# A third of each chunk's output products issued ahead, ten drains of TensorE removed, and a new order of all steps, in a delta-rule attention with a multiplicative feed-forward block

## The chip, the cores and the metric

The kernel runs on one core of a Trainium2 chip. The metric is the device time of one execution in microseconds (us). The kernel before took 578.32 us as the median of three runs (575.9 to 579.85). A profile shows one execution; times inside it are counted from its first instruction.

The engines are named as in the profile: PE is TensorE's matmul, PEld its load of weights (the stationary operand), DVE is VectorE, ACT is ScalarE, POOL is GpSimd, SP is SyncE, which here issues nearly all DMA transfers. A "q" behind an engine is its sequencer.

## The reference

Two blocks follow each other. The first is a delta-rule recurrence over 768 tokens for 4 batches of 8 heads with 48 features each; the second takes its output as 3072 tokens of 384 features.

```python
k_n = k / (np.linalg.norm(k, axis=-1, keepdims=True) + 1e-06)
for t in range(S):                       # S = 768
    kt, vt, bt = (k_n[:, :, t], v[:, :, t], beta[:, :, t, None])
    y[:, :, t] = np.einsum('bhd,bhde->bhe', q[:, :, t], state)
    v_old = np.einsum('bhde,bhd->bhe', state, kt)
    state = state + bt[:, :, :, None] * np.einsum('bhd,bhe->bhde', kt, vt - v_old)
x = y.transpose(0, 2, 1, 3).reshape(B * S, H * D)      # 3072 x 384
a = x @ w1                               # 384 x 1024
b = x @ w2                               # 384 x 1024
out = ((a * b) @ w3) @ w_out             # 1024 x 1024, 1024 x 384
```

q, k, v and beta come as 32-bit floats, the four weights as 64-bit floats, which the kernel turns into 32-bit floats on the chip.

## The kernel before

**Chunks.** The 768 tokens are 12 chunks of 64. Within a chunk the recurrence is written with matrices: scores between keys, the inverse of a triangular matrix made of them, and products with a state of 48 x 48 per batch and head that is handed from chunk to chunk. Two chunks make a pair u = 0 to 5 of 512 tokens for the feed-forward block.

**Steps.** Every piece of work is a Python generator that issues some instructions and then yields. A name in the string `ORDER` runs the generator of that name to its next yield, so `ORDER` is the program's order, written out by hand as some 1380 names. A name called past the generator's last yield does nothing. At the end `in_text_order` (L184) ties the instructions of each engine to that order, so each engine works through its own instructions strictly in the sequence of the text; between engines only semaphores hold, where data or a buffer demand it. The steps that matter here, with m a chunk and u a pair:

- `P0` to `P35` (`piece`, L758): load a piece of a 64-bit weight into one of five `raw` buffers (SP), convert it with two ScalarE operations, one VectorE and one GpSimd operation. P0-P7 are w_out, P8-P23 w3, P24-P35 w1 and w2. `t` transposes a piece of w3, `f` (`fold`, L833) multiplies w3 with w_out in two halves.
- `k`, `q`, `v`, `p`: loads of a chunk. `K`, `Q` and `d`: keys and queries transposed to features by tokens. `g`, `N`: norms of the keys.
- `s` (L426; `first_scores` for the first two chunks): for each half of a chunk's batches one group of products (L436, L442) and two VectorE evictions, U (L448) and PT (L459). `u` writes U to memory.
- `V` (`inverse`, L482): the inverse of two chunks together, 31 steps of two VectorE operations each (L502, L507), between a load `Ub<-Ud` and a store `Vd<-Vb`. For the first two pairs it works in a PSUM pair.
- `e` (`corner`, L538): loads the inverse's blocks (TT and T22), transposes one (L543) and completes the off-diagonal block with two groups of products (L560), each evicted by two ScalarE operations (L576, L587).
- `c` (`chain`, L605): three groups of products (L613): keys with the state, evicted as R (L647); R with the inverse, evicted as X (L658); X with the keys, evicted as the new state S (L679). R, X and S are one VectorE operation each.
- `y` (`outputs`, L685): the chunk's outputs, 64 matmuls in one step, of which 32 take X and PT ("of the tokens") and 32 take the state before the chunk and the queries, 16 for each of two halves z. A matmul of 32-bit floats is two instructions, so the profile shows 64 and 2 x 32. All 64 accumulate into one pair of banks. ScalarE then copies the pair into xT (L736), and six transfers move a part of xT between partitions (L747).
- `b`, `a` (`ab`, L850) and, for the last pair, `a50` to `a53` (`features`, L978): products with w1 and w2 (L857, L997), evicted by ScalarE and by a multiplication on VectorE (L869, L873).
- `S`, `o`, `x` (L916, L1066, L1114): sums of slabs on GpSimd (L930), seven groups of 16 products with the folded weights (L1089), and the results' additions and stores (L1118). Seven products take the place of eight, with sums beside them.

**PSUM.** There are eight banks. Four single banks turn under the tag "f" (`bank`, L172), two pairs under the tag "w" (`two_banks`, L169). `in_turn` (L141) gives the next index of the tag, and passes over an index that is in the set `held`; whoever gets a buffer waits until its last reader is done. Scores, corner, chain and outputs take their banks from "w"; weights, transposes, features and `o` take theirs from "f". The kernel before puts an index into `held` only in `inverse` for the first two pairs.

**The drain.** In `outputs` the products are in two lists: the first holds the state's products of half 0 and all products of the tokens, the second the state's products of half 1. Between the two lists TensorE drains:

```python
for mode, todo in enumerate(modes):
    if mode:
        drain = pe.drain().ins
    for h, z, r, lhs, rhs in todo:
        i = pe.matmul(region(h, z, r), lhsT=lhs, rhs=rhs, ...)
        issued[mode].append(i.ins)
        n += 1
for i in issued[0]:
    in_order(i, drain)
for i in issued[1]:
    in_order(drain, i)
```

Of the kernel before, what the change touches and what calls it, by code (L numbers as in the profile page):

```python
# [44 lines left out]
P14 V0 V0 V0 f0 P15 P15 P19 t11 f2 V0 P14 P14 V0 V0 V0 f1 f5 P23 P23 t6 V0 P15 P15 P23 t11 f5 f5 P23
t15 t15 h0 t7 f7 f7 t7 t6 f3 f3 V0 q2 P17 V0 V0 V0 V0 V0 V0 V0 V0 V0 P17 V0 k2 V0 V0 P16 P17 P28 P17
t9 P16 P24 v1 P16 P16 V0 V0 V0 V0 P28 P20 P28 P28 V0 g1 f3 t9 t8 k3 e0 f7 N0 N0 K2 h0 t8 f4 K2 P20
P20 e0 P20 t12 e0 K2 K2 t12 K2 Q2 n1 e0 e0 n0 n0 e0 P26 g1 f4 Q2 c0 Q2 Q2 f4 g1 g1 f6 Q2 n1 c0 c0
P24 P21 P24 P24 P21 P21 P21 c0 P26 P26 P26 g1 y0 y0 e1 e1 t13 K3 e1 t13 f6 K3 K3 K3 g1 e1 e1 f6 P29
g1 P25 g1 g1 P25 g1 K3 P25 y0 c1 c1 P25 b3 e1 c1 P27 b1 c1 y1 b3 P27 P27 b1 s2 P32 P32 b2 y1 b2 N1  # L50
s2 N1 N1 q3 Q3 P32 P27 P29 P29 s2 s2 Q3 Q3 P29 b4 P31 s2 s2 Q3 Q3 s3 s3 s3 s3 b4 y1 a01 P31 s3 u2
P32 V1 b6 s3 b0 a07 b0 P31 c1 a01 a04 b6 b7 a04 a07 c1 u3 V1 V1 V1 V1 V1 a05 a05 b5 b5 b7 a00 a06
a03 a02 c2 P30 a00 V1 V1 V1 V1 V1 V1 P30 P30 P30 P31 b3 V1 a06 a03 b1 a01 k4 P33 a02 V1 b0 V1 V1 P33
V1 V1 P33 P33 P34 V1 V1 b3 a00 V1 V1 V1 a01 b1 P34 b0 V1 a03 P34 P34 P35 P35 P35 P35 a04 b2 T V1 T
a00 V1 V1 V1 a03 V1 V1 V1 a06 T V1 k5 V1 V1 V1 V1 b5 V1 p4 a04 v2 n2 n2 b2 b4 b7 a06 b6 b5 a02 d4 b6
b4 p4 b7 a07 T a02 o0 a07 V1 e2 e2 e2 c2 e2 a05 e2 e2 c2 g2 g2 g2 g2 g2 g2 g2 e3 e3 e3 v3 e3 S0 g2
g2 a05 o0 x0 o0 d4 d4 d4 c2 y2 v4 x0 x0 S0 y2 g2 c2 S0 N2 p5 N2 k6 S0 o0 c2 n3 e3 e3 n3 c3 c3 N2 S0
S0 S0 S0 o0 S0 S0 S0 S0 S0 S0 S0 x0 c3 o0 c3 y3 s4 S0 x0 x0 o0 s4 y3 s4 s4 p5 x0 d5 d5 d5 d5 s5 s4
y3 u4 s4 s5 x0 s5 s5 s5 u5 a10 x0 V2 x0 x0 s5 a10 a12 a12 a12 a17 a17 a16 a12 a16 V2 V2 n4 V2 V2 V2
# [5 lines left out]
N3 x1 v8 x1 S1 o1 V3 x1 k9 V3 V3 V3 V3 V3 V3 x1 a27 a27 a22 a22 x1 a25 a25 V3 a23 V3 V3 a23 k8 p8 p8
V3 V3 V3 V3 V3 V3 V3 V3 a26 a26 a26 V3 V3 V3 a22 a26 a20 a20 a20 V3 V3 V3 V3 V3 V3 V3 V3 a21 a21 a22
d8 V3 g4 g4 g4 g4 g4 g4 g4 V3 a20 a27 a21 a21 a27 a24 a23 a24 c6 e6 e6 e6 g4 g4 g4 a25 d8 p9 e6 e6
e6 a24 c6 d8 d8 s8 a23 o2 v7 n7 N4 n8 n8 a25 N4 s8 c6 y6 s8 a24 o2 S2 c6 S2 y6 e7 e7 e7 x2 o2 e7 c6
e7 e7 x2 c7 S2 S2 o2 s8 p9 n7 c7 c7 S2 S2 S2 S2 o2 S2 x2 s8 s8 c7 d9 d9 S2 S2 y7 y7 u8 S2 S2 d9 S2
S2 d9 x2 o2 N4 s9 S2 x2 x2 s9 s9 s9 o2 s9 V4 s9 k11 c7 c7 y7 a32 a32 u9 x2 c8 x2 c8 V4 x2 a36 x2 a34  # L70
a34 a36 v10 a33 p10 a31 V4 a31 V4 V4 x2 V4 a33 a37 V4 V4 a30 v9 p10 V4 a37 a30 V4 V4 V4 V4 V4 V4 n9
n9 V4 V4 V4 V4 V4 V4 V4 V4 V4 V4 V4 V4 V4 V4 V4 a35 a35 a33 a33 V4 a35 a32 a30 V4 V4 V4 e8 d10 k10
e9 a32 a34 a30 a35 a36 e8 a31 e8 V5 a37 e8 e8 d10 p11 e8 d10 d10 p11 a34 S3 a36 g5 a31 S3 S3 o3 c8
e9 e9 g5 g5 x3 a37 o3 c8 c8 g5 c8 S3 e9 e9 o3 e9 c9 S3 g5 g5 g5 S3 g5 g5 S3 c9 S3 c9 S3 x3 o3 S3 S3
S3 g5 N5 S3 c9 y8 x3 S3 o3 d11 d11 y9 S3 d11 x3 o3 y8 d11 s11 S3 y9 y9 n10 n10 x3 x3 x3 x3 W x3 s11
s11 s11 s11 u11 s11 o3 x3 x3 s10 s10 s10 s10 s10 u10 s10 N5 N5 a47 a47 a47 a43 V5 a43 a42 a47 a40
a46 a45 V5 V5 V5 V5 V5 V5 V5 a42 V5 V5 V5 V5 V5 V5 V5 V5 V5 V5 V5 V5 V5 V5 a46 V5 V5 V5 a41 V5 V5
a40 a41 V5 V5 a44 a44 a44 V5 V5 a45 a40 V5 V5 a45 a44 e10 e11 a40 a46 c9 c9 a41 a43 c10 a45 e10 e10
a42 W W W W W a43 W W c10 v11 n11 n11 a41 e10 e10 a46 e10 S4 a42 o4 x4 e11 e11 o4 S4 S4 S4 S4 S4 S4
# [1197 lines left out]
```

## Time and profile before

| | |
|---|---|
| median of three runs | 578.32 us (575.9 to 579.85) |
| the profiled execution's own time | 578.96 us |
| its span, first to last instruction | 577.2 us |
| mean granted clock of TensorE | 0.979 |
| PE busy | 539.0 us, 8588 matmuls |
| PEld busy | 393.7 us |
| DVE busy | 340.6 us, 795 instructions |
| ACT busy | 144.8 us, 289 instructions |
| POOL busy | 171.6 us, 217 instructions |
| memory traffic | 43.09 MB read, 11.01 MB written, 94 GB/s over the span |

A line of the timeline or of a group names the line of the kernel, the engine, the operation, then the tile written and the tiles read, the shapes and the count. In a group's line there follow the busy time in all, the mean of one instruction in ns, and the idle time of the engine ahead of these instructions with what ended it. A matmul's end is modelled: matmuls overlap, so the time from one start to the next says how fast they issue. A wait is put down to the operation that ended it last.

### The profile page before, as it was taken

The page shows a single profiled execution, that of the slowest core. Times are in us where ns is not written, and L with a number is a line of the kernel's source. Part 1 is how long each engine was busy: PE and PEld are TensorE (multiplying, and loading weights), DVE is VectorE, ACT ScalarE, POOL GpSimd, SP SyncE. Part 2 cuts the span into 40 slices and gives each one's busy share as a digit, 9 for nine tenths or more (in the row PEclk, how much of TensorE's full clock was granted, in tenths as well). Part 3 has the DMA queues.
Part 4 walks back from the last instruction along what each step waited for, and adds up shares of the span by engine and source line. Part 5 has one row for each costly group of instructions (what it writes and reads, how often), then busy time and mean ns, then how long its engine had stood idle before and what let it go on. Part 6 is the DMA issues. An engine that isn't in the chain of part 4 may idle for free.

```text
span 577.2 us, 19704 instructions
## 1 busy us (share of the span) xinstructions
PE 539.0 (93%) x8588; PEld 393.7 (68%) x8588; DVE 340.6 (59%) x795; ACT 144.8 (25%) x289; POOL 171.6 (30%) x217
## 2 busy tenths in 40 slices
PE   4868998899899999998999999999999999989997
PEld 4734666787689744598744699444886446978897
DVE  6628824649774659865696616795455793123552
ACT  1766466534021011030111130110310102112210
POOL 7544253212838010431211090011840004810000
PEclk9579999999999999998999999999999999999999
DMA  9789964659564481534562534735504105010001
GB/s 183 231 268 257 202 158 117 147 125 172 101 111 79 74 158 32 102 49 74 134 102 65 76 53 76 151 43 110 75 13 91 37 36 85 17 50 8 0 1 55
DMA packets 202806, 56.57 MB, mean 98 GB/s; under 512 B 189952, under 2 KB 196096, under 8 KB 202720
## 3 DMA queue, kind: packets, MB, share of 16 engines
q1 hardware_dynamic: 200608, 54.92, 46.1%
q8 instruction: 67, 1.10, 0.8%
q10 hardware_dynamic: 2112, 0.39, 0.4%
q14 instruction: 19, 0.16, 0.1%
HBM read 43.09 MB, written 11.01 MB: 94 GB/s over the span
## 4 chain that ended last, share of the span: by engine, by line
PE 67%; DVE 13%; DMA 9%; SPq 5%; issue 3%; ACT 2%; POOL 1%; ACTq 0%; DVEq 0%; POOLq 0%
PE ps_f L857 26%; PE ps_f L1089 19%; DVE tb L502 5%; PE ps_w L613 5%; PE ps_f L997 4%; PE ps_w L718 4%; DMA raw<-in_moe_w_dram 3%; DVE ps_w L507 3%; PE ps_w L997 2%; PE ps_w L560 2%; DVE Vb L507 2%; PE ps_w L436 1%; PE ps_w L442 1%; SPq L762 1%; PE ps_f L366 1%
## 5 line engine op out<-in xcount | busy, mean ns | idle before, releaser
L857 PE MATMUL ps_f<-xT,w2s 128*128 128x512 f32 (+1 forms) x288 | 107.8, 525 | 4.0 <-DVE ab L873 2.6
L857 PE MATMUL ps_f<-xT,w1s 128*128 128x512 f32 (+1 forms) x288 | 107.3, 525 | 1.1 <-POOL w1s L777 0.6
L857 PEld LDWEIGHTS ps_f<-xT,w2s 128*128 128x128 f32 x288 | 53.7, 190 | 51.2 <-issue 42.8
L857 PEld LDWEIGHTS ps_f<-xT,w1s 128*128 128x128 f32 x288 | 53.7, 190 | 48.1 <-issue 43.2
L930 POOL TENSOR_TENSOR ab<-ab 128x256 f32<-128x256 f32 x80 | 55.5, 727 | 39.0 <-DVE ab L873 36.8
L1089 PE MATMUL ps_f<-w,ab 128*128 128x192 f32 x320 | 57.1, 332 | 1.6 <-DVE osb L1118 1.3
L869 ACT COPY ab<-ps_f 128x512 f32<-128x512 f32 (+1 forms) x48 | 23.8, 515 | 131.2 <-PE ps_f L857 121.4
L1089 PEld LDWEIGHTS ps_f<-w,ab 128*128 128x128 f32 x320 | 51.6, 190 | 2.8 <-issue 1.9
L836 PE MATMUL ps_f<-wo,w3T 128*128 128x384 f32 x128 | 46.0, 514 | 4.5 <-ACT w3T L830 3.6
L502 DVE TENSOR_TENSOR tb<-Vb,Ub 128x31 f32<-128x31 f32 (+15 forms) x124 | 43.4, 350 | 9.1 <-DMA Ub<-Ud 5.1
L507 DVE TENSOR_TENSOR Vb<-Vb,tb 128x31 f32<-128x31 f32 (+15 forms) x124 | 43.5, 351 | 4.3
L599 POOL TENSOR_TENSOR vtok<-vtok,n 128x384 f32<-128x384 f32 x24 | 19.6, 836 | 80.9 <-DMA vtok<-in_v_dram 78.0
L1089 PE MATMUL ps_f<-room,ab 128*128 128x192 f32 x240 | 43.0, 332 | 0.0
L873 DVE TENSOR_TENSOR ab<-ab,ps_f 128x512 f32<-128x512 f32 (+1 forms) x48 | 27.0, 589 | 21.5 <-PE ps_f L857 21.5
L836 PEld LDWEIGHTS ps_f<-wo,w3T 128*128 128x128 f32 x128 | 24.8, 200 | 21.2 <-issue 5.6
L1089 PEld LDWEIGHTS ps_f<-room,ab 128*128 128x128 f32 x240 | 38.6, 190 | 0.9
L298 POOL TENSOR_TENSOR sq<-ktok 128x384 f32<-128x384 f32 x24 | 19.7, 837 | 58.0 <-DMA out_dram<-osb 20.0
L576 ACT COPY T<-ps_w 32x512 f32<-32x512 f32 x24 | 13.8, 575 | 78.0 <-PE ps_w L560 55.3
L736 ACT COPY xT<-ps_w 112x256 f32<-112x256 f32 x48 | 14.3, 382 | 68.1 <-PE ps_w L718 68.1
L777 POOL TENSOR_TENSOR w<-w,raw 128x512 uint32<-128x512 uint32 x16 | 20.7, 1303 | 29.4 <-DVE w L775 17.6
L502 DVE TENSOR_TENSOR tb<-ps_w,Ub 128x31 f32<-128x31 f32 (+15 forms) x62 | 21.1, 340 | 4.3 <-ACT ps_w L496 2.7
L442 PE MATMUL ps_w<-KQ 48*64 48x64 f32 x640 | 23.5, 228 | 0.1
(148 smaller groups left out, 782.2 us busy)
## 6 DMA issues: line engine op xcount, KB each, us to landing
raw<-in_moe_w_dram SPq DMA_DIRECT2D x16, 512.0 KB, 6.5
vtok<-in_v_dram SPq DMA_DIRECT2D x24, 192.0 KB, 4.1
raw<-in_moe_w_dram SPq DMA_DIRECT2D x24, 192.0 KB, 3.9
out_dram<-osb SPq DMA_DIRECT2D x46, 96.0 KB, 2.5
ktok<-in_k_dram SPq DMA_DIRECT2D x44, 96.0 KB, 3.4
Ud<-U SPq DMA_DIRECT2D x48, 64.0 KB, 2.1
raw<-in_moe_w_out_dram SPq DMA_DIRECT2D x8, 384.0 KB, 5.6
Ub<-Ud SPq DMA_DIRECT2D x6, 512.0 KB, 4.1
```

The costliest lines, as they stand in the source:

```text
L442: pe.matmul(ps[half(z ^ j), 1, n + C * j : n + C * j + C], lhsT=x[:, 0, :], rhs=x[:, j, :], start=True, stop=True,)
L502: dve.tensor_tensor(out=tv, in0=V[:, 0 : s + 1, s : s + 1].to_broadcast([P, s + 1, n]), in1=U[:, s, s + 1 : BS].unsqueeze(1).to_broadcast( ...
L507: dve.tensor_tensor(out=o, in0=o, in1=tv, op=ALU.subtract)
L613: pe.matmul(out(ps, r, h, z), lhsT=lhs(r, h, z), rhs=rhs(r, h, z), start=True, stop=True,)
L718: i = pe.matmul(region(h, z, r), lhsT=lhs, rhs=rhs, start=part[n] not in part[:n], stop=part[n] not in part[n + 1 :],)
L836: pe.matmul(ps[:, 0:DM], lhsT=w3Ts[jc, kc // 4][:, kc % 4 * P : kc % 4 * P + P], rhs=wo(kc), start=(kc == 0), stop=(kc == KF - 1),)
L857: pe.matmul(ps[:].rearrange("p b c t -> p b (c t)"), lhsT=w[:, m, js], rhs=x[:, m, :, c0:c1].rearrange("p b c t -> p b (c t)"), start=(m = ...
L869: act.copy(out=t, in_=ps)
L873: dve.tensor_tensor(out=t, in0=t, in1=ps, op=ALU.mult)
L930: (dve if u == last else pool).tensor_tensor(out=o_, in0=x_, in1=y_, op=op)
L997: pe.matmul(ps[:, j, :], lhsT=w[j], rhs=x, start=first and j == 0, stop=j == 1, skip_group_check=not first,)
L1089: pe.matmul(ps[b][:, b, :], lhsT=ab_of(u, HF * f + i, t0), rhs=ws_[w][:, i], start=first and i == 0 and (b == 0 or n == "F"), stop=i == HF ...
```

## The change

`outputs` is written anew. For chunks 2 to 11 (`ahead`) it has one step more. The first step takes a pair of banks, puts it into `held` and issues the state's products of half 1. The second step issues all products of the tokens and then the state's products of half 0 into the same pair, with no drain. The third is the copies to xT, after which `held` is emptied. Chunk 1 does both groups in one step, with a drain in between; chunk 0 has no state and no drain. The products and their number are the same.

`ORDER` is replaced as a whole: the same steps with the ten new ones, 1389 names instead of 1379, differently mixed. Some places of it are shown below in both versions.

```diff
-V0 beta beta beta k0 g0 g0 g0 K0 K0 k1 K1 g0 g0 K0 K0 K1 K0 s0 g0 g0 g0 g0 K1 K1 K1 q0 Q0 Q0 Q0 g0
-N0 Q0 P8 P8 P8 q1 s0 s0 Q1 P8 s1 P12 P12 P12 Q1 Q1 Q1 Q1 h1 P12 P13 P13 Q0 t0 t4 P13 P13 t5 P10 P10
-P9 P9 P18 P18 P11 u0 P11 t0 t4 s1 s1 P0 P0 P10 P10 P9 P9 P18 P18 h0 t1 t2 t10 P11 t5 P11 t3 P0 P0 P2
+V0 beta beta P8 k0 P8 q0 k1 beta g0 K0 K0 g0 P11 P8 P18 P11 g0 K1 g0 g0 g0 g0 g0 K0 P12 g0 P18 q1
+P12 P11 g0 K1 Q0 K1 Q0 P2 P18 P2 P8 N0 P0 Q0 s0 P2 P0 s1 Q1 t0 P11 t3 P18 s0 P9 P2 P12 s0 P9 P10
+P0 P12 t0 Q1 P9 P10 P3 P1 s1 P10 P3 s1 h0 P0 t4 P3 P13 u1 Q1 t10 P9 P13 P1 t4 P7 P10 P13 h0 t3 P3
...
-N3 S1 c4 o1 S1 e5 S1 c4 y4 S1 S1 N3 S1 c4 p7 S1 d7 x1 p7 o1 y4 e5 e5 c4 d7 d7 d7 s7 s7 s7 s7 s7 s7
-c5 c5 c5 c5 s6 s6 s6 s6 s6 o1 u7 s6 y5 y5 v6 n6 n6 c5 x1 x1 o1 u6 c5 c6 V3 S1 V3 x1 y5 S1 x1 V3 S1
+S1 x1 e5 g3 c4 y4 S1 S1 p7 d6 e5 g3 c4 g3 c4 o1 N3 S1 Q3 S1 p7 S1 v6 y4 o1 d7 N3 y4 S1 n6 x1 S1 V3
+c4 e5 d7 x1 d7 c4 d7 e5 S1 o1 s7 s7 S1 S1 s7 s7 c5 s7 s7 c5 y5 c5 c5 s6 s6 S1 s6 s6 s6 o1 y5 N3 S1
...
-c10 S4 S4 S4 S4 S4 e11 e11 o4 x4 x4 e11 S4 c10 c10 S4 S4 S4 o4 y10 c10 c11 c11 y10 o4 x4 c11 c11 y11
-o4 x4 x4 o4 y11 y11 a50 X5 X5 x4 x4 X5 x4 x4 a51 a52 x4 a50 a50 a50 a50 a50 a50 a50 a50 a50 X5 a50
+e10 c10 x3 e10 a42 S4 e10 c10 S4 o4 W S4 e10 W S4 S4 x4 e11 W e11 e10 y10 e11 S4 o4 S4 S4 e11 c10
+c10 o4 e11 n11 e11 y10 S4 x4 o4 c10 y10 c10 c11 y11 o4 c11 x4 S4 c11 c11 S4 y11 S4 x4 S4 o4 y11 x4
...
     def outputs(c):
-        PT, St, X, KQ = PTs[c], Ss.get(c), Xs[c], KQs[c]
+        St, KQ = Ss.get(c), KQs[c]
         py = two_banks()
+
+        ahead = c > 1
+        if ahead:
+            held.add(("w", turns["w"]))
...
+        if c == 0:
+            accumulate(of_tokens(), True, True)
+        else:
+            issued = accumulate(of_state(1), True, False)
+            if ahead:
+                yield
+            else:
                 drain = pe.drain().ins
-            for h, z, r, lhs, rhs in todo:
...
-        for i in issued[0]:
-            in_order(i, drain)
-        for i in issued[1]:
-            in_order(drain, i)
+                for i in issued:
+                    in_order(i, drain)
+            issued = accumulate([*of_tokens(), *of_state(0)], False, True)
+            if not ahead:
+                for i in issued:
+                    in_order(drain, i)
         yield
...
+        if ahead:
+            held.clear()
         yield
```

`of_state(z)` and `of_tokens()` list the products as before, and `accumulate(todo, first, last_)` issues a list and marks the first and last product of each part of the banks as start and stop only where the list is the first or the last of the chunk.

More of the change, by code (lines that the diff above doesn't have):

```diff
@@ L45 @@
[L45 to L59, printed above, removed]
@@ L65 @@
[L65 to L79, printed above, removed]
```

94 lines of the change are left out of this document (64 added, 30 removed).

## The prediction

> **What bounds the kernel now.** I read the page first: span and busy shares.
>
> ```profile
> span 577.2 us, 19704 instructions
> ...
> PE 539.0 (93%) x8588; PEld 393.7 (68%) x8588; DVE 340.6 (59%) x795; ACT 144.8 (25%) x289; POOL 171.6 (30%) x217
> ```
>
> TensorE is idle for 577.2 - 539.0 = 38.2 us. Second, the busy time by stage (length of the stretch, then busy TensorE) says where.
>
> ```profile
> 101.30:150.00 48.70, 44.54 (x727) 36.56 (x724) 33.98 (x91) 19.14 (x42) 14.15 (x13) 1.00 0.74 147
> 150.00:571.00 421.00, 411.63 (x6421) 297.85 (x6421) 246.65 (x557) 69.18 (x142) 107.95 (x145) 1.00 0.36 67
> ```
>
> It idles 4.2 us from 101.3 to 150 and 9.4 us from there to 571. The other 24.6 us lie in the front, where the weights arrive, and in the last stores. Third, whom TensorE waited for (us in total, times, longest):
>
> ```profile
> PE ps_f L857 <- DVE ab L873: 2.6, 2, 1.3
> PE ps_f L857 <- POOL w2s L777: 1.4, 2, 0.9
> PE ps_w L613 <- DVE R L647: 1.4, 1, 1.4
> PE ps_f L1089 <- DVE osb L1118: 1.3, 1, 1.3
> PE ps_w L613 <- issue: 1.0, 1, 1.0
> PE ps_w L613 <- ACT TT L587: 1.0, 2, 0.7
> PE ps_w L718 <- DVE X L658: 0.7, 1, 0.7
> PE ps_w L436 <- DVE PT L459: 0.4, 1, 0.4
> PE ps_w L436 <- ACT TT L587: 0.3, 1, 0.3
> ```
>
> Behind the front the kernel is TensorE's own work with a dozen short waits. Six rows (L613, L718, L436) are small products of the recurrence that wait for their data or for the eviction of a "w" pair of banks: 1.4 + 1.0 + 1.0 + 0.7 + 0.4 + 0.3 = 4.8 us. A new order can win no more here than the waits hold, but it can add waits.
>
> **The change, part by part: the drains.** One chunk's output products on TensorE (start, duration), and the group row with the 216 ns of one product:
>
> ```profile
> 349.82 0.66 PE L718 MATMUL ps_w<-KQ,S 48*48 48x64 f32 x32
> 350.31 1.08 PE L718 MATMUL ps_w<-PT,X 64*48 64x64 f32 x64
> 351.50 0.66 PE L718 MATMUL ps_w<-KQ,S 48*48 48x64 f32 x32
> 352.10 2.87 PE L1089 MATMUL ps_f<-room,ab 128*128 128x192 f32 x16
> ```
> ```profile
> L718 PE MATMUL ps_w<-PT,X 64*48 64x64 f32 x768 | 13.3, 216 | 0.9 <-DVE X L658 0.7 <-issue 0.2
> ```
>
> The first 32 take 350.31 - 349.82 = 0.49 us of issue. The last of the 64 starts at 350.31 + 1.08 - 0.22 = 351.17, so a product could follow at 351.19; it comes at 351.50: a drain costs 0.31 us, and ten go, -3.1. The last 32 take 0.60 before a large product, 0.11 more than the first 32. The third that goes ahead is now a group of its own and may pay that 0.11 as well, 0 to +1.1 for ten; I take the middle, since such groups stand before small and before large products. Together **-2.6** (bounds -3.1 and -2.0). [...]
>
> **The hold.** With a third ahead, a pair of banks is held from y's first step to its copies. There are two pairs: meanwhile every product of chain, corner and scores takes the other, each behind the eviction of the one before. Nothing overtakes a waiting product: all of TensorE's queue stands behind it. Rows give the price of such a hand-over:
>
> ```profile
> 505.52 1.15 PE L613 MATMUL ps_w<-R,TT 64*64 64x48 f32 x64
> ...
> 506.49 0.63 PE L718 MATMUL ps_w<-KQ,S 48*48 48x64 f32 x32
> 506.81 0.96 DVE L658 TENSOR_TENSOR X<-ps_w,wt 128x768 f32<-128x768 f32 x1 [0.55 <-PE ps_w L613]
> 507.82 1.10 PE L718 MATMUL ps_w<-PT,X 64*48 64x64 f32 x59 [0.70 <-DVE X L658]
> ```
>
> L613 has issued by 506.49 and TensorE has X at 507.82: **1.33 us** for one VectorE operation of the chain (R, X or S), less what TensorE has in between (here 32 products, 0.49).
>
> ```profile
> 260.58 0.30 PE L436 MATMUL ps_w<-KQ 48*64 48x128 f32 x1
> ...
> 260.83 1.18 ACT L587 ACTIVATE TT<-ps_w 32x512 f32<-32x512 f32 x2 [3.09 <-PE ps_w L560]
> ...
> 261.81 0.69 DVE L448 TENSOR_TENSOR U<-ps_w,wt 128x512 f32<-128x512 f32 x1 [1.68 <-PE ps_w L442]
> 262.07 0.33 PE L436 MATMUL ps_w<-KQ 48*64 48x128 f32 x2 [0.32 <-ACT TT L587]
> ...
> 262.41 0.68 DVE L459 TENSOR_TENSOR PT<-ps_w,smask 128x512 f32<-128x512 f32 x1
> ```
> ```profile
> 501.94 1.19 ACT L736 COPY xT<-ps_w 112x256 f32<-112x256 f32 x4 [4.40 <-PE ps_w L718]
> ```
> ```profile
> 345.02 0.33 PE L436 MATMUL ps_w<-KQ 48*64 48x128 f32 x2
> ...
> 345.94 0.24 PE L613 MATMUL ps_w<-R,TT 64*64 64x48 f32 x2
> ```
>
> A corner's copies: the products before them had issued by 260.58, the pair is free at 262.07, **1.49**. y's copies are as long (1.19), so 1.49 too. A score group issues for 345.94 - 345.02 = 0.92; one that starts at 260.58 is done at 261.50 and its two evictions at 262.41 + 0.68 = 263.09, **1.6**.
>
> I went through both orders, noted for every step of chain, corner, scores and outputs the pair it takes by the turns and holds of `in_turn` (L141), and what TensorE has in between. Short in the new order are: e1 c1, nothing between, 1.49; e2 y2 c2 (0.49 between), 1.0; y3 s4 on the pair just copied, 1.49, then s5 s4 s5 in turns, 0.7 + 0.4; e5 y4 c4, 1.0; e7 s8 c7, 0.6; e8 y8 e8, 1.0; y9 s11 s10, 0.6; e10 y10 e11, 1.0; c10 c11, 1.33; c11 y11, 1.33; and "s7 s7 c5 s7 s7 c5 y5 c5 c5 s6 s6 S1 s6 s6 s6", where y5 holds one pair while c5's last product and both groups of s6 share the other: 0.7 + 0.2 + 0.6 + 1.3 + 1.6 = 4.4. Sum 16.3. The old order by the same prices: e2 c2 1.5, e2 e3 0.5, s4 s5 0.4, e5 s7 0.6, s7 c5 0.7, c5 c5 1.3, c9 c9 1.2, c11 y11 0.8, sum 7.0, of which the waits show 4.8, a share of 0.69. I take the same share: 0.69 x 16.3 = 11.2, **+6.4** (bounds +2, if only 0.42 of it shows, and +11.5, if all is paid).
>
> **VectorE's backlog in V1.** The 2.6 us behind ab are feature products whose bank waits until VectorE is past steps of the second inverse, two operations each:
>
> ```profile
> L502 DVE TENSOR_TENSOR tb<-ps_w,Ub 128x31 f32<-128x31 f32 (+15 forms) x62 | 21.1, 340 | 4.3 <-ACT ps_w L496 2.7
> ```
>
> At 0.7 us a step the old order has ten bank turns with 4.5 us of products against 5 to 10 us of VectorE; the new one mixes finer and has two, 6.2 and 5.5 against 4.5. **-2.0** (bounds 0 and -2.6). The 1.4 us for w2s stay: its pieces keep their place.
>
> **The front.**
>
> ```profile
> 71.66 1.07 ACT L511 COPY Vb<-ps_w 128x512 f32<-128x512 f32 x2 [3.31 <-DVE ps_w L507]
> ...
> 86.61 1.15 PE L613 MATMUL ps_w<-vtok,TT 64*64 64x48 f32 x64
> 87.68 2.85 PE L836 MATMUL ps_f<-wo,w3T 128*128 128x384 f32 x8
> ...
> 96.43 4.29 SPq L747 DMA_DIRECT2D xT<-xT  x6
> ...
> 101.31 0.70 PE L857 MATMUL ps_f<-xT,w1s 128*128 128x256 f32 x2
> ```
> ```profile
> raw<-in_moe_w_dram SPq DMA_DIRECT2D x16, 512.0 KB, 6.5
> ```
>
> Ahead of c0's first product (86.61) TensorE has the same steps in both orders, differently mixed; SP issues 24 weight pieces ahead of V0's last step in the old order, 25 in the new. Past queues: on SP, P8 before q0 and k1 delays chunk 1's keys, and N0 stands behind P18 on VectorE; u1 and u0 with fewer pieces ahead give that back. On ScalarE P21's conversion now stands between e0's two copies, and P21 (512 KB, 6.5 from issue to landing as the median of its kind) is issued behind the loads of e0, so it lands later than e0's first copy: I put c0 up to 3 us later. In return xT's transfer (96.43 to 101.31, 4.9) has a corner product, half a fold (2.85) and c1's first product over it, where it had c1's alone: up to -3. I take **0** (bounds -4, if V0's start, with 14 pieces ahead instead of 15, stays earlier, and +3).
>
> **At nothing** I cost the tail from S5 on (the same products in line behind the same waits), osb's 1.3 (o4's last two groups still follow each other) and the earlier starts of V2 to V5, whose transfers feature products hide; a us missing there would lie on the path.
>
> **Sum.** The profiled execution took 578.96 (span 577.2 and 1.8 around it), 0.64 above the median of the runs. 578.96 - 2.6 + 6.4 - 2.0 + 0 = 580.8; beside the median, **580.1**, +0.3%. About 1%, 5.8 us, is what a measurement can tell from no change.
>
> **The rivals.** (1) Faster, the engines run ahead where my walk keeps them in step: of the added hand-overs half goes (-3.2), V0 stays early (-4), w2s goes (-1.4): 571.5. For it: only 0.69 of the old prices was seen. Against it: the front is where transfers bind. (2) Slower: the held pair costs all it can. The granted clock (third number from the end) is its second half:
>
> ```profile
> 264.00:266.00 2.00, 0.61 (x35) 0.48 (x26) 1.83 (x3) 0.00 (x0) 0.00 (x0) 1.00 0.23 33
> ...
> 267.00:268.00 1.00, 1.00 (x39) 1.00 (x36) 0.63 (x1) 0.00 (x0) 0.00 (x0) 0.50 0.60 99
> ...
> 269.00:270.00 1.00, 1.00 (x38) 1.00 (x35) 0.85 (x2) 0.00 (x0) 0.00 (x0) 0.50 1.19 194
> ```
>
> After 1.4 us idle out of 2, amid small products, the clock is at half from 267 to 270: 1.5 lost. The new order has three such stretches (s7 to s6; y3 s4 s5; c10 to y11), the old one the first alone. Two more dips are 3.0, all prices paid 11.5 - 6.4 = 5.1: 588.2. It decides from about 11 us of added waits on. [...] (3) The change doesn't save its drains: the third that goes ahead pays as much at its new place: 582.7. Against it: between groups of different kinds the rows leave no gap. (4) The front is late, c0's 3 us with nothing back: 583.1.
>
> **How the numbers follow.** Forecast 0.47; (1) 0.16; (2) 0.25; (3) 0.05; (4) 0.07. Faster by over 1% (below 572.5): (1) without its upper end, 0.14. Slower (above 584.1): (2) and a part of the forecast and (4), 0.32. Within: 0.54. The range leaves out the outer half of (1) and a quarter of (2): 571.5 to 590.
>
> **What would show it.** Right: no gap before the last L718 group in chunks 2 to 11; waits of L613, L560, L436 and L718 on R, TT, T, PT and xT that sum to 9 to 13 us, the most of it between s7 and s6; less of L857 behind ab; first features at 98 to 104 us. Wrong: a first feature product far from 101 (the front decides), waits below 6 us (products there don't queue as I walked them), or granted clock at half in several slices.

## The result and the profile after

The changed kernel takes 592.34 us as the median of four runs (591.29 to 595.32), beside 577.11 us for the kernel before; the ratio is 1.025, with a 95% interval of 1.0208 to 1.0291. It is slower, above the forecast of 580.1 and above the upper end of the range, 590. The profiled execution took 591.98 us, 13.0 us more than the one of before. The rows below are from it. Its lines stand a little lower than before's: the chain's products are L614, the corner's L561, the scores' L437, the outputs' L722, the features' L878, the output pieces' L1110 with their additions at L1139.

The page's first rows:

```profile
span 590.3 us, 19686 instructions
...
PE 543.7 (92%) x8588; PEld 397.9 (67%) x8588; DVE 336.7 (57%) x795; ACT 143.6 (24%) x289; POOL 171.9 (29%) x217
```

TensorE issues the same 8588 products, is busy 4.7 us longer and idle 46.6 us instead of 38.2. Ten drains less and more busy time do not fit together unless products ran slower or overlapped less somewhere; we come back to that.

Where the time comes from is seen when the stretches are cut at equal work. These are busy times by stretch, with the length first, then busy TensorE and its count of products. Cuts: first fold, first product of the chain (c0), first feature product. Before:

```profile
0.00:36.50 36.50, 20.90 (x557) 19.11 (x558) 19.82 (x46) 18.43 (x34) 22.52 (x35) 0.79 0.85 216
36.50:86.60 50.10, 46.63 (x404) 28.49 (x403) 31.09 (x85) 28.71 (x54) 21.50 (x21) 0.95 0.91 217
86.60:101.30 14.70, 12.89 (x473) 9.53 (x472) 6.62 (x12) 9.32 (x19) 5.51 (x6) 1.00 0.49 116
```

After:

```profile
0.00:41.00 41.00, 24.20 (x557) 21.19 (x558) 23.45 (x49) 21.02 (x40) 24.14 (x37) 0.94 0.80 214
41.00:91.00 50.00, 45.76 (x404) 28.02 (x403) 29.98 (x83) 26.32 (x49) 20.17 (x19) 0.98 0.93 209
91.00:108.00 17.00, 14.22 (x406) 10.48 (x407) 5.30 (x9) 8.99 (x18) 6.81 (x6) 0.90 0.53 115
```

The same 557 products take 41.0 us instead of 36.5, the next 404 the same 50 us, and the third stretch 2.3 us more with 67 products fewer. The first feature product comes at 107.50 us instead of 101.31. So a good half of the loss is there before the feed-forward block has begun, in the part that I had costed at nothing. (In a second profiled execution of the same kernel the front's part was smaller, 3.7 us by the table below, and the whole as long.)

Behind it, the waits of TensorE from 104 to 571 us (us in total, times, longest):

```profile
PE ps_f L878 <- ACT ab L890: 2.5, 3, 1.7
PE ps_w L437 <- DVE PT L460: 2.4, 3, 1.4
PE ps_f L1110 <- DVE osb L1139: 1.8, 2, 1.3
PE ps_w L437 <- ACT xT L755: 1.7, 2, 1.3
PE ps_w L614 <- ACT TT L588: 1.3, 3, 0.7
PE ps_w L614 <- DVE S L680: 1.2, 1, 1.2
PE ps_w L722 <- DVE X L659: 1.1, 1, 1.1
PE ps_w L437 <- DVE X L659: 1.1, 1, 1.1
PE ps_w L561 <- ACT T L577: 0.8, 1, 0.8
PE ps_w L561 <- ACT TT L588: 0.8, 1, 0.8
```

The waits of the small products (L437, L614, L561, L722) on evictions, with four rows of 0.4 to 0.7 not shown here, sum to 12.5 us, and to 13.8 with those that the profile puts to "issue"; before, the same kinds sum to 5.3 with "issue". The forecast had 11.2 for them. The old row for VectorE's backlog in V1 (2.6 us behind `ab`, on VectorE) is gone; 2.5 us behind ScalarE's half of `ab` have come instead.

To follow the time from stage to stage I use one number, TensorE's **lag**: the start of a step's first product in the timeline, less TensorE's own work issued ahead of it (each step counted at a fixed duration from rows like those of the prediction; an output at 2.28 us, without its drain at 2.05). It can be compared at equal work however the steps are ordered. The columns are 80 us of work (first chain steps), 130 (end of V1), 225 (ahead of s7), 250 (behind y5), 540 (the end).

| kernel | ratio to before | first feature product | 80 | 130 | 225 | 250 | 540 |
|---|---|---|---|---|---|---|---|
| before | 1 | 101.3 | 28.1 | 29.9 | 29.1 | 33.0 | 29.0 |
| changed | 1.025 | 107.5 | 35.3 | 34.9 | 38.5 | 46.5 | 44.2 |
| changed, again | 1.026 | 104.3 | 31.8 | 34.0 | 36.8 | 46.1 | 43.4 |
| old front | 1.011 | 98.0 | 23.9 | 27.6 | 30.6 | 38.3 | 36.6 |
| new front alone | 1.019 | 105.7 | 33.0 | 40.1 | 39.1 | 43.4 | 39.2 |
| k1 first | 1.017 | 101.8 | 29.0 | 29.9 | 33.0 | 42.2 | 39.8 |
| old order to the first fold | 1.014 | 98.3 | 26.0 | 29.5 | 32.4 | 40.6 | 37.9 |
| order alone, old outputs | 1.024 | 108.9 | 37.0 | 37.5 | 39.6 | 42.9 | 44.2 |
| y5 late | 1.013 | 105.8 | 36.2 | 36.1 | 39.2 | 43.3 | 40.5 |
| old front and y5 late | 1.005 | 99.2 | 25.1 | 27.5 | 31.6 | 34.7 | 33.0 |
| the same, two more hand-overs | 1.009 | 102.4 | 28.3 | 31.6 | 34.8 | 37.8 | 34.3 |
| third ahead in the old order | 1.022 | 104.2 | 30.3 | 31.7 | 36.0 | 38.7 | 45.5 |
| three pieces moved in the kernel before | 1.000 | 100.1 | 26.8 | 31.9 | 30.9 | 33.9 | 32.6 |
| two pieces moved | 0.999 | 101.1 | 27.0 | 30.9 | 29.9 | 33.0 | 29.8 |

The ledger of the changed kernel against before, from the first two rows: +7.2 up to 80 us of work; -2.2 from there to the end of V1; +10.2 from there to the end (of which +4.4 ahead of s7, +4.1 from s7 to y5, the rest behind); and 2.3 us less work without the drains. 7.2 - 2.2 + 10.2 - 2.3 = 12.9, and the spans differ by 13.1.

### The profile page after: what moved, and what is told of

It reads as the page before. It is cut to its first block, busy times and chain, and to the rows that moved or that the text cites. A ratio compares the mean times of both kernels' runs of the same rounds, so it can differ in the third digit from the quotient of the medians.

```text
span 590.3 us, 19686 instructions
## 1 busy us (share of the span) xinstructions
PE 543.7 (92%) x8588; PEld 397.9 (67%) x8588; DVE 336.7 (57%) x795; ACT 143.6 (24%) x289; POOL 171.9 (29%) x217
## 4 chain that ended last, share of the span: by engine, by line
PE 69%; DMA 9%; DVE 6%; SPq 6%; issue 3%; ACT 3%; POOL 2%; ACTq 0%; POOLq 0%; DVEq 0%
PE ps_f L878 29%; PE ps_f L1110 17%; PE ps_w L614 4%; PE ps_f L1018 4%; PE ps_w L722 3%; DMA raw<-in_moe_w_dram 3%; PE ps_w L1018 2%; PE ps_w L561 2%; DMA ktok<-in_k_dram 2%; SPq L259 2%; PE ps_w L437 2%; SPq L783 2%; PE ps_w L443 1%; DMA Ud<-U 1%; DMA Vd<-Vb 1%
## 5 line engine op out<-in xcount | busy, mean ns | idle before, releaser
L878 PE MATMUL ps_f<-xT,w2s 128*128 128x512 f32 (+1 forms) x288 | 106.7, 524 | 1.7 <-ACT ab L890 1.7
L878 PE MATMUL ps_f<-xT,w1s 128*128 128x512 f32 (+1 forms) x288 | 107.4, 525 | 0.8 <-ACT ab L890 0.8
L878 PEld LDWEIGHTS ps_f<-xT,w2s 128*128 128x128 f32 x288 | 54.1, 190 | 48.3 <-issue 42.3
L878 PEld LDWEIGHTS ps_f<-xT,w1s 128*128 128x128 f32 x288 | 53.7, 190 | 46.6 <-issue 41.9
L1110 PE MATMUL ps_f<-w,ab 128*128 128x192 f32 x320 | 57.5, 332 | 1.9 <-DVE osb L1139 1.8
L1110 PEld LDWEIGHTS ps_f<-w,ab 128*128 128x128 f32 x320 | 51.5, 190 | 3.5 <-issue 2.1
L508 DVE TENSOR_TENSOR Vb<-Vb,tb 128x31 f32<-128x31 f32 (+15 forms) x124 | 44.8, 361 | 4.3
L299 POOL TENSOR_TENSOR sq<-ktok 128x384 f32<-128x384 f32 x24 | 19.9, 839 | 91.0 <-DMA out_dram<-osb 36.1
L1110 PE MATMUL ps_f<-room,ab 128*128 128x192 f32 x240 | 45.0, 343 | 0.0
L1110 PEld LDWEIGHTS ps_f<-room,ab 128*128 128x128 f32 x240 | 40.6, 198 | 1.0
L577 ACT COPY T<-ps_w 32x512 f32<-32x512 f32 x24 | 13.8, 575 | 92.2 <-PE ps_w L561 86.1
L798 POOL TENSOR_TENSOR w<-w,raw 128x512 uint32<-128x512 uint32 x16 | 20.9, 1310 | 26.3 <-DVE w L796 13.3
L449 DVE TENSOR_TENSOR U<-ps_w,wt 128x512 f32<-128x512 f32 x20 | 13.6, 686 | 24.5 <-PE ps_w L443 24.1
L437 PE MATMUL ps_w<-KQ 48*64 48x128 f32 x320 | 21.8, 281 | 5.1 <-DVE PT L460 2.4
```

The costliest lines, as they stand in the source:

```text
L437: pe.matmul(ps[half(z), 0, n : n + 128], lhsT=x[:, 0, :], rhs=x.rearrange("p j t -> p (j t)"), start=True, stop=True,)
L508: dve.tensor_tensor(out=o, in0=o, in1=tv, op=ALU.subtract)
L798: pool.tensor_tensor(out=du, in0=du, in1=lo, op=ALU.add)
L878: pe.matmul(ps[:].rearrange("p b c t -> p b (c t)"), lhsT=w[:, m, js], rhs=x[:, m, :, c0:c1].rearrange("p b c t -> p b (c t)"), start=(m = ...
L1110: pe.matmul(ps[b][:, b, :], lhsT=ab_of(u, HF * f + i, t0), rhs=ws_[w][:, i], start=first and i == 0 and (b == 0 or n == "F"), stop=i == HF ...
```

## Experiments on the front

**Old front.** The order of before up to the first step of V1, then the changed order.

```diff
-V0 beta beta P8 k0 P8 q0 k1 beta ... (changed order up to the first V1)
+V0 beta beta beta k0 g0 g0 g0 K0 ... (order of before up to the first V1)
 V1 ... (changed order, without the steps already done)
```

> The order of before up to the first step of V1 (about 110 us), then the changed order with the steps that are left; the new outputs function. Theory (the front of the new order costs 7.3 us by the first feature product, 107.5 against 101.3 us in the traces plus 1.1 us less TensorE work done, and nothing later makes it up): 592.3 - 7.3 = 585.0 us, first feature product at about 101 us. If the 2.3 us that V1's stretch gained in the changed kernel go with the front's order of conversions, up to 587.3. Rival (TensorE would wait in V1 for VectorE anyway, so the late front is made up there and the loss is all hand-overs): 591 to 593 us.

Measured: 585.82 us, ratio 1.0108 (1.0077 to 1.0138); the changed kernel stands at 1.025. The lag at the end is 7.6 us less than the changed kernel's, and it is 7.3 less already at the end of V1. So the front's loss is real and stays.

**New front alone.** The opposite: changed order up to V1, then the order and the outputs function of before.

```diff
-V0 beta beta beta k0 g0 g0 g0 K0 ... (order of before up to the first V1)
+V0 beta beta P8 k0 P8 q0 k1 beta ... (changed order up to the first V1)
 V1 ... (order of before, without the steps already done)
```

> The changed order up to the first step of V1, then the order of before with the steps that are left; the outputs function of before, with its drains. Theory (the front alone costs 7.3 us): 577.1 + 7.3 = 584.4 us, 582 if the gain of 2.3 us in V1's stretch comes along. Rival (a late front is hidden behind V1's elimination on VectorE): 577 to 578 us, with the waits of V1's stretch shorter by what the front lost.

Measured: 589.47 us, ratio 1.0185 (1.012 to 1.025), 10.7 us above before and more than either theory. The table says why: 4.9 us of lag at 80 us of work grow to 10.2 in V1's stretch. The old order of V1 does not go with the new front; the new one, behind the same front, took up 0.4 us there, and added 2.2 in the second execution (changed, again: 31.8 to 34.0). Hence the 2.2 us that V1 "gained" in the changed kernel are no gain that can be had alone: behind the old front the new order of V1 adds 2.4 to 3.7 us of lag from 80 to 130 in three executions, the old one 1.4 to 5.1 in four.

**k1 first.** Only the first steps of the changed order change places.

```diff
-V0 beta beta P8 k0 P8 q0 k1 beta g0
+V0 beta beta k0 k1 q0 P8 P8 beta g0
```

> The changed kernel; only the first steps change places: the loads of chunk 1's keys (k1) and of the first queries (q0) go to SP's queue ahead of the first piece of w1 (P8) instead of behind it. In the trace of the changed kernel k1's keys were issued at 8.07 us (before: 2.48), V0's Ub load at 41.5 (38.1), and the first fold started at 40.6 (36.1). Theory (the first 4.5 us of the late front come from k1's place in that queue): first fold at about 37 us, 592.3 - 3.5 = 588.8 us, 587.5 to 590. Rival (the fold's start hangs on ScalarE's own order, where the w3T copies stand behind weight pieces that wait for their DMA, 3.0 us at 33.9): 591.5 to 592.5 us, first fold still at about 40.

Measured: 589.71 us, ratio 1.0167 (1.0102 to 1.0231). SP's queue (start and duration of an issue, then the operation) in the changed kernel,

```profile
8.07 2.70 SPq L231 DMA_DIRECT2D ktok<-in_k_dram  x4
...
41.52 0.34 SPq L489 DMA_DIRECT2D Ub<-Ud  x1
```

and with k1 first (P8, which k1 passes, is a piece of w3):

```profile
2.47 2.79 SPq L238 DMA_DIRECT2D ktok<-in_k_dram  x4
...
39.37 0.34 SPq L496 DMA_DIRECT2D Ub<-Ud  x1
```

Chunk 1's keys are issued 5.6 us earlier and V0's load 2.2 us earlier; c0's first product moves from 91.05 to 87.6 and the first feature product from 107.50:

```profile
107.50 0.48 PE L878 MATMUL ps_f<-xT,w1s 128*128 128x256 f32 x1
```

to 101.75.

The time agrees with the theory, its way does not: the first fold stays at 40.7 us, as the rival had it. So there seem to be two threads. The fold hangs on ScalarE's order, where copies of w3T stand behind weight pieces; the chain hangs on chunk 1's keys by way of V0. The fold's lateness was hidden, the chain's was not. How much the places of these few names carry is known roughly: 4.8 us by the ratios, whose intervals overlap a little (1.0102 to 1.0231 against 1.0208 to 1.0291), and by the lag at 80 us 6.3 against the first execution of the changed kernel, 2.8 against the second and 5.7 against the mean of the five below. I take some 5 of the front's 7 us. Of the 5.75 us at the first feature product 3.4 are there at c0; the rest is a stop inside chunk 0's outputs, 1.49 us here and 2.20 in the changed kernel, and a stretch at half clock behind the longer one (the 0.90 of its third stretch).

**The old order up to the first fold** (36 us), then the changed order.

```diff
-V0 beta beta P8 k0 P8 q0 k1 beta ... (changed order up to the first fold)
+V0 beta beta beta k0 g0 g0 g0 K0 ... (order of before up to the first fold)
 f0 ... (changed order, without the steps already done)
```

> The order of before up to its first fold (36 us), then the changed order with the steps that are left. Theory (of the 7.3 us the first 4.5 arise ahead of the first fold, and stay): 592.3 - 4.5 = 587.8 us, first feature product at about 103 us. Rival 1 (the loss arises between the first fold and the first feature product, in the new order of the chain's first steps): 592 us. Rival 2 (all of the front's loss begins ahead of the fold): 585 us.

Measured: 588.49 us, ratio 1.0141 (1.0076 to 1.0206). The first feature product comes at 98.3, earlier than expected, and the lag at 80 is at the old front's level (26.0). So all of the front's loss begins ahead of the first fold (rival 2) by the trace, although of the 9.3 us of lag that are won there V1 takes 3.9 back. The profiled execution was the fastest of the four, at 585.74 us; the median stands where the theory had it. This order of V1 seems to be paced by something other than TensorE, which no run isolates: what the front wins beyond some point is not kept.

The front is also the part that varies. Seven profiled executions with the old order ahead of V1 have a lag at 80 of 23.9 to 30.3 (mean 27.1), five with the changed order 31.8 to 37.0 (mean 34.7). The difference of the means, 7.6, rests on twelve executions; a single one of these numbers is good to 3 us.

## Experiments on the held pair and the order

**Order alone.** The changed order with the outputs function of before: no third ahead, nothing held, the drains back.

```diff
-e2 g2 T S0 y2 e3 d4 p5 c2 g2 v4 c2 ... (and the first y of every chunk from 2 to 11)
+e2 g2 T S0 e3 d4 p5 c2 g2 v4 c2 ...
```

> The changed order with the outputs function of before: the early third is taken back, each output's products are one group with its drain at the place of the second part. Theory (the held pair's own part of the hand-overs is about 5 us of the some 9 us that the rest of the order lost, and the ten drains come back with 2.6): 592.3 - 5.0 + 2.6 = 589.9 us, 588.5 to 591. Rival 1 (the hand-overs come from the new order and not from the hold): 594.9 us. Rival 2 (all of the 9 us are the hold's): 592.3 - 9 + 2.6 = 585.9 us.

Measured: 593.68 us, ratio 1.0237 (1.0167 to 1.0307): as slow as with the third ahead. Of its 6.7 us of lag from V1 to the end (37.5 to 44.2; changed kernel 9.3, before -0.9) none is a hold's. So of the 10.2 us that the changed kernel loses there, up to 7.6 belong to the new order by itself and at least 2.6 to the hold. But this execution has a stretch at half clock (third number from the end) where no other trace here has one, with TensorE busy throughout:

```profile
415.69:419.10 3.41, 3.41 (x5) 1.01 (x3) 1.78 (x4) 0.49 (x1) 1.77 (x3) 0.50 0.39 56
```

That is 1.7 us lost. Without it the order's share is 5.9 and the hold's 4.3; each is read from one execution. Not that the hold is harmless: ahead of s7 it costs 1.5 us (3.6 against 2.1) and from s7 to y5 4.7 (8.0 against 3.3). Behind y5 the lag falls by 2.3 with the thirds ahead and grows by 1.3 without them; 1.7 of this difference is the clock's, and at most the other 1.9 are waits that the thirds fill. My price list was near in its sum and wrong in its title: well over half of what this stretch lost is there without any hold. And the measured times, 592.34 with the thirds and 593.68 without, leave the third ahead at about nothing: what its hold costs, its drains give back.

**y5 late.** The changed kernel, but chunk 5 in one group with its drain.

```diff
-        ahead = c > 1
+        ahead = c in (2, 3, 4, 6, 7, 8, 9, 10, 11)
 ...
-s7 s7 c5 y5 c5 c5 s6 s6 S1 s6 s6 s6 o1 y5
+s7 s7 c5 c5 c5 s6 s6 S1 s6 s6 s6 o1 y5
```

> The changed kernel, but chunk 5's outputs in one group with a drain, as before, so that no pair is held while s7, c5 and s6 run; the order of all other steps stays. Theory (the held pair alone costs 5 us in this block: with the old outputs function the changed order lost 2.8 us from s7 to y5, with the new one 7.6): 592.3 - 4.7 = 587.6 us. Rival (the gaps come back behind the block, since VectorE is what is late there): 591 to 592 us.

Measured: 587.6 us, ratio 1.0128 (1.0088 to 1.0168), the theory's number. The block's waits in the changed kernel (268 to 292 us),

```profile
PE ps_w L437 <- DVE PT L460: 1.4, 1, 1.4
PE ps_w L437 <- DVE X L659: 1.1, 1, 1.1
PE ps_f L1110 <- DVE osb L1139: 0.5, 1, 0.5
PE ps_w L614 <- DVE PT L460: 0.5, 1, 0.5
PE ps_w L614 <- DVE R L648: 0.4, 1, 0.4
```

and with y5 late (266 to 290; L621 is the chain, L1117 the output pieces):

```profile
PE ps_w L621 <- DVE R L655: 1.1, 1, 1.1
PE ps_w L621 <- DVE PT L467: 0.5, 1, 0.5
PE ps_f L1117 <- DVE osb L1146: 0.5, 1, 0.5
```

3.9 against 2.1 us: the scores' waits on PT and X, 2.5 us, are the held pair's, and a wait on R of 1.1 instead of 0.4 is what y5's third had filled. The lag grows by 4.1 us here instead of 8.0; of the 2.1 us that the waits don't account for, some 1.3 go with the clock, which is at half for 6.8 us in the changed kernel and for 3.4 here (below); the rest is open.

**Both together**: old front and y5 late.

```diff
-V0 beta beta P8 k0 P8 q0 k1 beta ... (changed order up to the first V1)
+V0 beta beta beta k0 g0 g0 g0 K0 ... (order of before up to the first V1)
 ...
-        ahead = c > 1
+        ahead = c in (2, 3, 4, 6, 7, 8, 9, 10, 11)
```

> The order of before up to the first step of V1, then the changed order, and chunk 5's outputs in one group with a drain: the two causes found so far undone together. Theory (the front's 7 us and the held pair's 4 us between s7 and y5 are separate, so they add): 585.8 - 4 = 581.8 us, 580.5 to 583; what is left against before, some 4 us, are hand-overs at y3/s4, e8/e9 and c11/y11. Rival (one of the two hides behind the other): 585 us.

Measured: 580.87 us, ratio 1.0053 (1.0018 to 1.0087). The two causes add (by the lag at the end 7.6 and 3.7 us alone, 11.2 together), and leave 0.5%.

**Two more hand-overs undone** on top of that. In this kernel the moved seventh piece of unit 0 stands ahead of the last three of that unit's sums of slabs, so it computes with sums that aren't finished; the work is the same.

```diff
-y3 y3 x0 s4 S0 y3 s5 s4 s4 s5 ... S0 x0 o0
+y3 o0 y3 x0 s4 S0 y3 s5 s4 s4 s5 ... S0 x0
 ...
-e11 y10 S4 x4 o4 c10 y10 c10 c11
+e11 y10 c10 y10 o4 S4 x4 c10 c11
```

> The run with the old front and chunk 5 late, and two more hand-overs of the changed order undone: the seventh output piece of unit 0 goes between chunk 3's outputs and the scores that want the held pair (s4, s5), and chunk 10's product for S goes ahead of the fourth piece of unit 4 instead of right ahead of chunk 11's R. Theory (they close 1.29 + 0.46 of waits at 190 to 197 us with the half clock behind them, some 0.8, and 1.24 at 503 us): 580.9 - 3.8 = 577.1 us, ratio 0.997 to 1.001 to before: what remains of the changed order is then no slower than before. Rival (a closed wait opens again at the next wait for VectorE or a transfer): 580 to 581 us.

Measured: 582.2 us, ratio 1.0085 (1.005 to 1.012), no better. The trace shows both. From 130 us of work to the end the lag grows by 2.7 us instead of 5.5, so the hand-overs do close, although 1.9 us open at the next feature product; but the profiled execution came out of the front 4.1 us later with the same order there. This one is inconclusive.

**The third ahead in the old order.** Nine chunks get the new outputs function in the order of before; where a neighbour would want the held pair, it is moved. Two of the nine places:

```diff
-x0 c3 o0 c3 y3 s4
+x0 y3 c3 o0 c3 y3 s4
 ...
-a24 c6 d8 d8 s8 a23 o2 v7 n7 N4 n8 n8 a25 N4 s8 c6 y6 s8 a24 o2
+a24 y6 c6 d8 d8 c6 a23 o2 s8 v7 n7 N4 n8 n8 a25 s8 y6 N4 s8 a24 o2
```

> The order of before with the new outputs function in nine chunks (2 to 4 and 6 to 11; chunk 5 keeps its drain): the held group stands right ahead of the chain's product for X, and the few steps that would want the held pair (e3, e5, s8, e9, e11) are moved behind a 2.8 us output piece. Theory (a drain is worth 0.25 to 0.31 us of TensorE, and a held pair costs nothing where a 2.8 us piece stands behind each hand-over): 577.1 - 9 x 0.28 = 574.6 us, 573.9 to 575.5. Rival 1 (drains cost nothing of their own, the wait for X takes their place): 577 us. Rival 2 (a held pair costs in itself, whatever stands beside it): 580 us or more.

Measured: 592.53 us, ratio 1.0215 (1.015 to 1.028). The theory and the first rival missed. The second rival's "580 us or more" covers the time, but not the way: chunk 3, where no neighbour moved, loses nothing (the lag is 37.5 ahead of it and 37.3 behind). The blocks in which neighbours moved opened waits that were not there before, from 0.4 us around chunk 4 to 5.4 around chunks 6 and 7. Around chunk 2 (165 to 195 us; L1117 are output pieces, L621 the chain):

```profile
PE ps_f L1117 <- ACT room L1150: 1.8, 1, 1.8
PE ps_w L621 <- ACT xT L762: 1.3, 1, 1.3
```

and around chunks 6 and 7 (326 to 372 us):

```profile
PE ps_f L1117 <- DVE ab L901: 3.6, 2, 1.9
PE ps_f L1117 <- DVE room L1146: 1.8, 1, 1.8
```

The pieces that were to cover the hand-overs wait themselves: moving X's eviction ahead on VectorE puts `ab` and the pieces' additions behind it, and e3's copies ahead on ScalarE put `room` behind them. A place in one queue is a place in three.

**Pieces into hand-overs of the kernel before.** Three output pieces move.

```diff
-s7 s7 c5 c5 c5 c5 s6 s6 s6 s6 s6 o1 u7 s6 y5
+s7 s7 c5 c5 o1 c5 c5 s6 s6 s6 s6 s6 u7 s6 y5
 ...
-g5 S3 c9 S3 c9 S3 x3 o3
+g5 S3 c9 x3 o3 S3 c9 S3
 ...
-c11 c11 y11 o4 x4 x4 o4
+c11 c11 o4 y11 x4 x4 o4
```

> The kernel before, its outputs function and drains as they were; three output pieces of 2.87 us are moved into hand-overs: the fifth of unit 1 between chunk 5's R and its product for X (1.39 us of wait in before's trace, and slow matmuls behind it until 270.5 us), the fourth of unit 3 between chunk 9's R and X (1.04), the sixth of unit 4 between chunk 11's X and its outputs (0.70, and 1.33 ahead of the seventh). Theory (a hand-over costs what stands open in it, and a piece that was needed anyway closes it for nothing): the waits go, -1.4 -1.0 -2.0, and the half clock behind the first of them with some 1.2: 577.1 - 5.6 = 571.5 us, 570.5 to 573.5. Rival (each piece leaves an equal gap at the place that it left): 577 us.

Measured: 579.44 us, ratio 1.0001 (0.9968 to 1.0033). The three waits are gone; two others stand for them (478 to 525 us; L1005 are the last features, L568 the corner):

```profile
PE ps_f L1005 <- DMA xT<-xT: 2.5, 1, 2.5
PE ps_w L568 <- DVE T L551: 2.0, 1, 2.0
```

The first is mine: with the sixth piece ahead of them, chunk 11's outputs are copied and sent 2.9 us later, and the last features wait for the transfer. The second is a transfer that landed later: the inverse's blocks of V5 were loaded 4.65 us behind the issue of their store (473.66 and 478.31 us), before 3.36 (473.53 and 476.89). A stop of 1.3 us that the profile puts to "issue" came inside chunk 5's outputs. Without that third move,

```diff
-g5 S3 c9 S3 c9 S3 x3 o3
+g5 S3 c9 x3 o3 S3 c9 S3
 (and the first of the three moves; chunk 11 as before)
```

> The kernel before with two of the three moved pieces: the fifth of unit 1 between chunk 5's R and X, the fourth of unit 3 between chunk 9's R and X. The third, which put chunk 11's outputs 2.9 us later and opened a wait of 2.45 us for their transposed copy and its transfer, is taken back. Theory (what those two closed, 2.7 and 1.2 us by the trace, stays closed, less up to 1.6 where a wait opened inside chunk 5's outputs): 1.2 to 3.9 us below before, ratio 0.993 to 0.998. Rival (transfers and VectorE, which are not moved, set what follows, and the gain is given back): ratio 1.000.

Measured: 577.26 us, ratio 0.999 (0.9965 to 1.0015). The 1.39 and 1.04 us of wait are closed in its trace, and the time cannot be told from before's. The rival holds, and its trace shows two things that gave gain back: the late transfer is there again (4.67 us, and a wait of 1.8 behind it), and so is the stop in chunk 5's outputs (1.0). So neither was a chance of one execution; why the transfer takes longer with these moves is open. No version here beats the kernel before.

**The changed kernel again**, unchanged, as a second measurement:

> The changed kernel as it is, beside the other runs on one chip, so that the ratios stand on the same runs of before. Every theory: ratio 1.025 to before, 1.021 to 1.029.

Measured: 591.52 us, ratio 1.026 (1.0211 to 1.031).

## Why the prediction was wrong

**The step that failed is the front.** It was put at 0 (bounds -4 and +3), because "u1 and u0 with fewer pieces ahead give that back". They did not: the front costs 7.2 us in the first pair of traces, 7.6 in the mean of twelve executions, and roughly 5 of it hang on one place that the prediction had named, "P8 before q0 and k1 delays chunk 1's keys". I saw that delay (5.6 us in the traces) at the head of a chain (keys, norms, U, V0, corner, c0) and let it be paid back by the number of pieces further down in the queue, without walking that chain through VectorE and ScalarE. With the front at 7.2 the same sum gives 587.3 beside the median and 588.0 for the profiled execution, which took 591.98. Of the 4.0 us beyond, 3.8 are a second, smaller miss, the term of the hand-overs (10.2 for 6.4).

**Drains: right.** -2.6 was forecast. Chunk 7 in the changed kernel:

```profile
358.77 0.66 PE L722 MATMUL ps_w<-KQ,S 48*48 48x64 f32 x32
359.25 1.10 PE L614 MATMUL ps_w<-R,TT 64*64 64x48 f32 x64
...
363.08 1.11 PE L722 MATMUL ps_w<-PT,X 64*48 64x64 f32 x64
364.01 0.63 PE L722 MATMUL ps_w<-KQ,S 48*48 48x64 f32 x32
364.57 1.24 PE L1110 MATMUL ps_f<-room,ab 128*128 128x192 f32 x6
```

The third takes 0.48 us of issue, the rest 1.49, together 1.97 where it was 2.28: 0.31 less. Counted at 2.05 an output, the lag runs flat over chunks 6 and 7 (44.0 to 44.3), so ten are worth 2.3 to 3.1.

**Hand-overs: near in the sum of waits, wrong in the cause.** 9 to 13 us of such waits were to be seen, "the most of it between s7 and s6"; 12.5 were, and 3.4 of them there, about a quarter. They grew by 8.5 against the 6.4 of the forecast, and the clock's longer dip behind them (1.3 us) makes most of the difference to 10.2. But the cause given, the held pair, carries 2.6 to 4.3 of the 10.2 us; the order carries the rest, with or without it.

**V1: right in size by luck** (-2.2 for -2.0). The waits behind VectorE's backlog went as forecast, but 2.2 of the 2.5 us behind ScalarE's half of `ab` came in their place in this stretch; and the 1.4 us for w2s, which were to stay, went. In the second execution of the changed kernel V1 added 2.2 us of lag, 0.4 more than before's, and behind the old front the new order gains nothing there. What the kernel gained in the first execution goes with its late front.

**The rivals.** The second came nearest: the hand-overs with one more dip of the clock, at the place that it named (s7 to s6), though not at the two others. With the front's 7 us added instead of 0 it would have stood at 595. "The front is late by 3" had the right place at less than half its size. The sum of both, each a part of it, was nowhere among the cases: I let them exclude each other.

**The signs to watch** were right where they spoke: the first feature product came outside 98 to 104 us, and the front decided half of the loss. But the waits, the other sign, came out as for a right forecast: they can't tell the hold from the order.

## What to carry over

Walk a moved load to the first instruction on TensorE that needs it, through every queue in between; a delay at the head of that chain (5.6 us for chunk 1's keys) wasn't paid back here by a shorter queue further down. In a program that orders each engine by one text, a step that is moved takes its place in all queues: a piece moved to cover one wait opened another in most places tried here. A split that frees one engine for 0.3 us and holds a buffer for several is to be priced at the hand-overs it serialises, and where it stands first: here, put ahead of a wait, it filled it (1.1 us behind R became 0.4), and put ahead of a row of scores it nearly doubled the block's waits (2.1 us became 3.9).
